# Opening four rows of the first MLP product on half their contraction, with all weight loads ahead of step 4 and step 2 of the attention in two parts

## The chip, the cores and the metric

The kernel runs on one core of a Trainium2 chip. The metric is the device time of one execution in microseconds (us). Most executions of one kernel lie within some tenths of a microsecond of each other, and the change is about an effect of that size, so the number of runs and their range are given with each median.

Engines are called by short names in the profile: PE is TensorE (PEld its weight loads), DVE VectorE, ACT ScalarE, POOL GpSimd, SP or SPq SyncE, which here issues the loads and most stores.

## The reference, cut to what matters

A blocked linear attention with decay (4 batches, 8 heads, 768 positions, head size 64) feeds an MLP with a tanh-GELU:

```python
for b in range(nb):                       # blocks of 64 positions
    intra = einsum('bhic,bhjc->bhij', qb, kb) * Dmask          # decay mask
    intra = einsum('bhij,bhjd->bhid', intra, vb)
    inter = einsum('bhid,bhde->bhie', qb * lam_pow, kv_state)
    out[:, :, sl] = intra + inter
    kv_state = lam_block * kv_state + einsum('bhsd,bhse->bhde', kb_dec, vb)
...
x = attn_out.transpose(0, 2, 1, 3).reshape(3072, 512)          # tokens x model
h = x @ w_in                                                   # 512 -> 2048
g = 0.5 * h * (1 + tanh(c * (h + 0.044715 * h**3)))
return g @ w_out                                               # 2048 -> 512
```

## The kernel before

The attention runs in 24 steps. A step is 256 positions of one batch for one half of the heads (step 0: positions 0 to 255, heads 0 to 3; step 1: the same positions, heads 4 to 7; step 2 and 3: the next 256 positions; and so on). Each step loads q, k and v, casts them to 16 bits (`prep`), transposes q and k on PE and evicts them (`stage_t`), and then multiplies (`region`): scores on PE, times the mask on DVE, times v on PE, plus the running state. Its result, `xT`, holds model dimensions on partitions: the 512 model dimensions are four chunks of 128, and one head half fills two of them. So a token group can enter the MLP only when both of its steps are through.

The MLP is cut into *fillers*, which keep PE busy between the parts of the attention. The first group has 512 tokens, 16 rows of the first product and 16 parts of the second:

```python
def mm1(f0):                       # one row: four products of 512 columns, then GELU on ScalarE
    Hps = ps_M.tile([P, per, N], FP32, tag="M", name="Hps")
    for i in range(per):
        f = f0 + i
        for c in range(NC):
            pin(nc.tensor.matmul(Hps[:, i, :], w_in16[:, c, f * P : (f + 1) * P],
                                 x[:, c, :], start=(c == 0), stop=(c == NC - 1)))
    pin(nc.scalar.activation(out=gT[:, f0 : f0 + per, :], in_=Hps[:], func=AF.Gelu_apprx_tanh))

def mm2(tau, part):                # one part: four products of 512 columns
    ...
    for f in range(4 * part, 4 * part + 4):
        pin(nc.tensor.matmul(O2[tau][:], gT[:, f, tau * P : (tau + 1) * P],
                             w_out16[:, f, :], start=(f == 0), stop=(f == NF - 1)))
    if part < 3:
        return
    ...
    pin(nc.vector.tensor_copy(out=o32[:], in_=o2[:]))      # VectorE empties the output
    pin(nc.sync.dma_start(out=dst, in_=o32[:]))
```

The order of loads on SyncE and the order of work at the start (`idle(n)`: n dummy products on a constant, `R(n, s)`: scores of step n and products of step s, `U(n)`: second state update, `fill(n)`: n fillers):

```python
for s in range(4): load_step(s)
for j in range(4): load_win(j)          # quarters of w_in, 1 MB each
load_wout(0); load_wout(1); load_step(4)
load_wout(2); load_wout(3); load_step(5)
for s in range(6, 9): load_step(s)
...
R(2, 1); stage_t(3); idle(3)
R(3, 2, split=True); idle(3)
R(None, 3)
cast_win(0); U(2); U(3)
...                                      # the other casts
fill(17)                                 # 16 rows and one part
prep(4); cast_wout(2); cast_wout(3); stage_t(4)
fill(3);  R(4, None); U(4); prep(5)
fill(4);  stage_t(5); prep(6)
fill(2);  R(5, 4); U(5)
fill(2);  stage_t(6); prep(7)
fill(2);  R(6, 5); U(6)
...
```

Of the kernel before, what the change touches and what calls it, by code (L numbers as in the profile page):

```python
# [15 lines left out]
def kernel(  # L16
# [12 lines left out]
    P = 128  # L29
# [14 lines left out]
    wst = ctx.enter_context(tc.tile_pool(name="wst", bufs=4))  # L44
# [31 lines left out]
    def load_win(j):  # L76
        t = wst.tile([P, NC, 512], FP32, tag="w32", name=f"wi32_{j}")
        pin(nc.sync.dma_start(out=t[:], in_=moe_w_in[:, j * 512 : (j + 1) * 512].rearrange(
            "(c p) f -> p c f", p=P)))
        wstage[("i", j)] = t  # L80
# [7 lines left out]
    def cast_win(j):  # L88
        t = wstage.pop(("i", j))
        w = 128 if j == 0 else 256  # L90
        for i in range(0, 512, w):
            pin(nc.vector.tensor_copy(out=w_in16[:, :, j * 512 + i : j * 512 + i + w],
                                      in_=t[:, :, i : i + w]))
# [15 lines left out]
    for j in range(4):  # L109
        load_win(j)  # L110
    load_wout(0)
    load_wout(1)
    load_step(4)
    load_wout(2)
    load_wout(3)
    load_step(5)
    for s in range(6, 9):
        load_step(s)
# [61 lines left out]
    def prep(s):  # L180
        half = s % 2
        q32, k32, v32 = ld32.pop(s)
        hs = slice(half * HH, (half + 1) * HH)

        def wide(t):
            return t.rearrange("p j h d -> p h j d")

        def decay(t):
            return t[:, hs, :].unsqueeze(3).to_broadcast([P, HH, 2, D])

        tqk = a16p.tile([P, 2, 2, HH, D], FP16, tag="qk16", name=f"qk16_{s}")
        tq, tk = tqk[:, 0], tqk[:, 1]
        tv = a16p.tile([P, 2, HH, D], FP16, tag="v16", name=f"v16_{s}")
        q_eng = nc.gpsimd if s == 3 else nc.vector
        pin(q_eng.tensor_tensor(wide(tq), q32[:], decay(dq), ALU.mult))  # L195
        if s == 0:
            inverse(halves[0])
            odd(halves[1])
            inverse(halves[1])
        pin(nc.scalar.activation(out=wide(tk), in_=k32[:], func=AF.Copy))  # L200
        pin(nc.gpsimd.tensor_tensor(wide(tv[:]), v32[:], decay(dv), ALU.mult))  # L201
        a16[s] = (tq, tk, tv)
        if s >= FIRST_DMA_T:
            o = qkp.tile([P, 2, 2, 2, P], FP16, tag="qkT", name=f"qkT_{s}")
            pin(nc.sync.dma_start_transpose(out=o[:].rearrange("p a j h t -> p (a j h) t"),
                                            in_=tqk[:].rearrange("p a j h d -> p (a j h d)")))
            qkT[s] = o
        if s >= 6:
            load_ahead(s + 3)

    def stage_t(s):
        if s >= FIRST_DMA_T:
            return
        tq, tk, _ = a16[s]
        Tps = ps_M.tile([P, 2, 2, 2, P], FP16, tag="M", name="Tps")
        for i, t in enumerate((tq, tk)):
            for hp in range(2):
                for j in range(2):
                    pin(nc.tensor.transpose(Tps[:, i, j, hp, :], t[:, j, 2 * hp : 2 * hp + 2, :],  # L219
                                            ident[:]))  # L220
        o = qkp.tile([P, 2, 2, 2, P], FP16, tag="qkT", name=f"qkT_{s}")
        if 1 <= s <= 3:
            pin(nc.scalar.activation(out=o[:], in_=Tps[:], func=AF.Copy))  # L223
        else:
            pin(nc.vector.tensor_copy(out=o[:], in_=Tps[:]))
        qkT[s] = o
# [10 lines left out]
    def region(n, s, split=False):  # L237

        OK = [ps_M.tile([P, 512], FP32, tag="M", name=f"OK{c}") for c in range(2)]
        opened = set()  # L240
# [7 lines left out]
        if n is not None:  # L248
            o = qkT[n]
            _, tk, tv = a16[n]  # L250
            Sps = ps_S.tile([P, 2, 2, 2, P], FP32, tag="S", name="Sps")

            def scores():
                for hp in range(2):
                    for jk in range(2):
                        for hl, c in TILES:
                            pin(nc.tensor.matmul(  # L257
                                Sps[half64(c), hl, hp, jk, :],
                                o[half64(hl), 1, jk, hp, half64(c)],
                                o[half64(hl), 0, :, hp, half64(c)], start=True, stop=True,  # L260
                                skip_group_check=True))

            def products():
                last = (n // 2) % NSB == NSB - 1
                for jk in range(2):
                    for hp in range(2):
                        for c, hl in TILES:
                            if c == 1 and last:
                                continue
                            pin(nc.tensor.matmul(  # L270
                                OK[c][half64(hl), 256 + hp * D : 256 + hp * D + D],
                                tk[half64(c), jk, 2 * hp + hl, :],
                                tv[half64(c), jk, 2 * hp + hl, :],
                                start=start(c, hl), stop=(jk == 1), skip_group_check=True))
                Kps[n] = OK

            if split:
                products()
                update(n, 0)
                scores()  # L280
            else:
                scores()
                products()
            PT = []
            for hps in ([slice(0, 1), slice(1, 2)] if split else [slice(0, 2)]):
                w = hps.stop - hps.start
                t = ptp.tile([P, 2, w, 2, P], FP16, tag=f"PT{w}", name=f"PT_{n}_{hps.start}")
                for src, dst in ([(Sps[:, :, hps.start], t[:, :, 0])] if split else
                                 [(Sps[:].rearrange("p a b c d -> p (a b) c d"),
                                   t[:].rearrange("p a b c d -> p (a b) c d"))]):  # L290
                    pin(nc.vector.tensor_tensor(  # L291
                        dst.rearrange("p a c d -> p a (c d)"),
                        src.rearrange("p a c d -> p a (c d)"),
                        mask[:].unsqueeze(1).to_broadcast([P, 2 * w, 2 * P]), ALU.mult))
                PT += [t[:, :, i] for i in range(w)]
            PTs[n] = PT
        if s is None:
            return
# [4 lines left out]
        for hp in range(2):  # L303
            for jk in range(2):
                for c, hl in TILES:
                    pin(nc.tensor.matmul(  # L306
                        OK[c][half64(hl), hp * P : hp * P + P], tv[half64(c), jk, 2 * hp + hl, :],
                        PT[hp][half64(c), hl, jk, :], start=start(c, hl), stop=False,
                        skip_group_check=True))
        ins = ins_of.pop(s)  # L310
        for c in range(2):
            u = ins[c]
            if u is None:
                continue
            for hp in range(2):
# [13 lines left out]
    ins_of = {}  # L329

    def update(s, c):
# [3 lines left out]
        if c == 0:  # L335
            ins_of[s] = [state[half][1] if sb > 0 else None, None]
# [3 lines left out]
        OK = Kps[s] if c == 0 else Kps.pop(s)  # L340
        K = OK[c][:, 256:384].rearrange("p (hp d) -> p hp d", hp=2)
        t = ucp.tile([P, 2, D], FP32, tag=f"t{half}", name=f"t_{s}_{c}")
        if sb == 0 and c == 0:
            pin(nc.vector.tensor_copy(out=t[:], in_=K))
        else:
            for hp in range(2):
                pin(nc.vector.scalar_tensor_tensor(  # L347
                    t[:, hp, :], state[half][0][:, hp, :],
                    lamu[:, 2 * half + hp : 2 * half + hp + 1], K[:, hp, :], ALU.mult, ALU.add))
        bd = ubp.tile([P, 2, 2, D], FP16, tag=f"u{half}", name=f"u_{s}_{c}")  # L350
        pin(nc.gpsimd.tensor_tensor(  # L351
            bd[:], t[:].unsqueeze(2).to_broadcast([P, 2, 2, D]),
            lumask[:, 2 * half : 2 * half + 2, :].unsqueeze(3).to_broadcast([P, 2, 2, D]),
            ALU.mult))
        state[half] = (t, bd)
        if c == 0:
            ins_of[s][1] = bd
# [6 lines left out]
    def queue_group(g):  # L364
# [3 lines left out]
        x = xT.pop(g)  # L368
# [45 lines left out]
        for f in range(0, NF, per):  # L414
            filler.append(lambda f=f: mm1(f))
# [22 lines left out]
    def R(n, s, split=False):  # L438
        region(n, s, split)
        if s is not None and s % 2 == 1:  # L440
            g, i = group_of[s // 2]
            if i == len(groups[g]) - 1:
                queue_group(g)
        if n is not None and not split:
# [6 lines left out]
    idle(12)  # L451
# [13 lines left out]
    R(1, 0)  # L465
# [3 lines left out]
    U(1)  # L469
    prep(3)  # L470
    R(2, 1)
    stage_t(3)
    idle(3)
    R(3, 2, split=True)
    idle(3)
    R(None, 3)
    cast_win(0)
    U(2)
    U(3)

# [4 lines left out]
    fill(17)  # L485
    prep(4)
    cast_wout(2)
    cast_wout(3)
    stage_t(4)
    fill(3)  # L490
    R(4, None)
    U(4)
    prep(5)
    fill(4)
    stage_t(5)
    prep(6)
    fill(2)
    R(5, 4)
    U(5)
    fill(2)  # L500
    stage_t(6)
    prep(7)
    fill(2)
# [57 lines left out]
```

## Time and profile before

| | before |
|---|---|
| time, median (range, runs) | 214.66 us (214.61 to 215.03, 4 runs) |
| span of the profiled run, and that run's time | 213.5 us, 215.29 us |
| first row of the MLP / fifth row | 19.69 us / 23.61 us |
| first part of the second product | 33.97 us |
| scores of step 5 | 45.47 us |
| tail: last DVE copy through to end of span | 3.25 us |

The tail is counted here and below from the end of the drain record that DVE has behind its last copy, 0.05 us after the copy itself.

The page of the kernel before gives busy time by engine (us, share of the span, instructions) and the chain of work that ended last:

```profile
PE 205.1 (96%) x2118; PEld 107.0 (50%) x2118; DVE 91.3 (43%) x179; ACT 94.2 (44%) x175; POOL 64.2 (30%) x82
...
PE 86%; DMA 7%; SPq 2%; ACT 2%; DVE 1%; issue 0%; ACTq 0%
```

PE is busy for 96% of the span, and the chain runs through it. What is left to win is idle time and dummy products at the start, and the few waits around the first attention steps behind the first MLP group.

### The profile page before, as it was taken

To read this page: it belongs to the slowest core of one execution; us is meant where nothing else is said; L and a number is where in the kernel's file an instruction comes from. 1 tells how busy PE (TensorE), PEld (TensorE's weight loads), DVE (VectorE), ACT (ScalarE), POOL (GpSimd) and SP (SyncE) were. 2 spreads that over 40 slices of the span, in tenths; PEclk is the share of its full clock that TensorE was granted. 3 is DMA by queue.
4 is the path that set the end of the run, shared out by engine and by line. 5 is a ranking of instruction groups with operands and counts; after the bars stand their busy time and mean duration, and the time that the engine had idled before them with its cause. 6 is when DMAs were issued, how large, how long until landed. Compare 5 with 4: busy or idle time off the path is not lost.

```text
span 213.5 us, 5059 instructions
## 1 busy us (share of the span) xinstructions
PE 205.1 (96%) x2118; PEld 107.0 (50%) x2118; DVE 91.3 (43%) x179; ACT 94.2 (44%) x175; POOL 64.2 (30%) x82
## 2 busy tenths in 40 slices
PE   7879999999999999999999999999999999999993
PEld 2444444455875784444455455444455454444452
DVE  4887522478784523740464541363632241100121
ACT  2375774342672471477420577420576211475000
POOL 5493136454582333422421320432420110000000
PEclk9999999999999999999999999999999999999999
DMA  5999999999999999893675673615120012100112
GB/s 135 301 331 391 383 352 370 286 288 325 303 221 223 309 208 253 221 227 71 176 211 144 205 194 69 180 53 150 49 52 0 0 52 98 54 0 0 49 63 86
DMA packets 61879, 37.82 MB, mean 177 GB/s; under 512 B 17696, under 2 KB 54816, under 8 KB 61856
## 3 DMA queue, kind: packets, MB, share of 16 engines
q1 hardware_dynamic: 61696, 37.37, 63.4%
q8 instruction: 16, 0.26, 0.5%
q10 hardware_dynamic: 160, 0.13, 0.2%
q14 instruction: 7, 0.06, 0.1%
HBM read 27.27 MB, written 6.29 MB: 157 GB/s over the span
## 4 chain that ended last, share of the span: by engine, by line
PE 86%; DMA 7%; SPq 2%; ACT 2%; DVE 1%; issue 0%; ACTq 0%
PE Hps L376 38%; PE O2ps L387 34%; DMA k<-in_k_dram 7%; PE Sps L257 3%; PE OK L316 3%; PE OK L306 3%; SPq L67 2%; PE O2ps L407 2%; PE Tps L219 1%; PE OK L270 1%; ACT qkT L223 1%; ACT xT L324 1%; ACT qk L200 1%; DVE PT L291 0%; PE idle L432 0%
## 5 line engine op out<-in xcount | busy, mean ns | idle before, releaser
L376 PE MATMUL Hps<-xT,w_in 128*128 128x512 f16 (+1 forms) x448 | 86.0, 349 | 0.3 <-ACT xT L324 0.3
L387 PE MATMUL O2ps<-w_out,gT 128*128 128x512 f16 x368 | 82.9, 379 | 0.0
L378 ACT ACTIVATE gT<-Hps 128x512 f16<-128x512 f32 x96 | 57.3, 596 | 34.5 <-PE Hps L376 33.7
L376 PEld LDWEIGHTS <-w_in 128*128 128x128 f16 x448 | 43.3, 98 | 38.1 <-issue 0.6
L351 POOL TENSOR_TENSOR u<-t,lumask 128x256 f16<-128x256 f32 x40 | 27.9, 706 | 91.1 <-DVE t L347 64.2
L387 PEld LDWEIGHTS <-gT 128*128 128x128 f16 x368 | 35.3, 98 | 39.7
L291 DVE TENSOR_TENSOR PT<-Sps,mask 128x1024 f16<-128x1024 f32 (+1 forms) x25 | 29.4, 1180 | 45.2 <-PE Sps L257 45.2
L324 ACT ACTIVATE xT<-OK 128x256 f16<-128x256 f32 x48 | 18.3, 451 | 51.3 <-PE OK L316 39.5
L394 DVE COPY o<-O2ps 128x512 f32<-128x512 f32 x23 | 15.8, 690 | 52.6 <-PE O2ps L387 52.5
L201 POOL TENSOR_TENSOR v<-v,dv 128x512 f16<-128x512 f32 x24 | 25.9, 1081 | 4.7 <-DMA v<-in_v_dram 4.6
L195 DVE TENSOR_TENSOR qk<-q,dq 128x512 f16<-128x512 f32 x23 | 19.7, 859 | 6.9 <-DMA q<-in_q_dram 6.9
L200 ACT ACTIVATE qk<-k 128x512 f16<-128x512 f32 x24 | 15.0, 623 | 9.3 <-DMA k<-in_k_dram 9.3
L347 DVE SCALAR_TENSOR_TENSOR t<-t,lamu,OK 128x64 f32<-128x64 f32 x64 | 14.5, 274 | 2.4 <-PE OK L270 1.4
L432 PE MATMUL idle<-ones 128*128 128x512 f16 x30 | 10.2, 479 | 1.5 <-DVE ones L126 1.5
L257 PEld LDWEIGHTS <-qkT 64*64 64x64 f16 x384 | 6.1, 106 | 10.1 <-issue 6.8
L257 PE MATMUL Sps<-qkT 64*64 64x128 f16 x384 | 10.0, 222 | 0.9 <-ACT qkT L223 0.7
L103 POOL CAST w_out<-wo 128x1024 f16<-128x1024 f32 x6 | 6.6, 1113 | 12.4 <-DMA wo<-in_moe_w_out_dram 12.4
L306 PE MATMUL OK<-PT,v 64*64 64x128 f16 x384 | 10.2, 218 | 0.0
L316 PE MATMUL OK<-qkT,u 128*128 128x128 f16 x80 | 8.6, 222 | 0.0
L219 PE MATMUL Tps<-ident,qk 128*128 128x128 f16 x72 | 6.1, 221 | 2.2 <-DVE qk L195 1.0
L306 PEld LDWEIGHTS <-v 64*64 64x64 f16 x384 | 6.8, 108 | 0.9 <-issue 0.8
L219 PEld LDWEIGHTS <-qk 128*128 128x128 f16 x72 | 4.6, 99 | 5.0 <-DVE qk L195 1.8
(34 smaller groups left out, 54.4 us busy)
## 6 DMA issues: line engine op xcount, KB each, us to landing
q<-in_q_dram SPq DMA_DIRECT2D x24, 256.0 KB, 4.7
k<-in_k_dram SPq DMA_DIRECT2D x24, 256.0 KB, 4.9
v<-in_v_dram SPq DMA_DIRECT2D x24, 256.0 KB, 5.2
out_dram<-o SPq DMA_DIRECT2D x23, 256.0 KB, 2.7
wi<-in_moe_w_in_dram SPq DMA_DIRECT2D x4, 1024.0 KB, 11.4
wo<-in_moe_w_out_dram SPq DMA_DIRECT2D x4, 1024.0 KB, 9.4
qkT<-qk SPq DMA_TRANSPOSE x15, 3.4
out_dram<-o SPq DMA_DIRECT2D x1, 96.0 KB, 2.2
```

The lines of the kernel that those rows point to most:

```text
L195: pin(q_eng.tensor_tensor(wide(tq), q32[:], decay(dq), ALU.mult))
L200: pin(nc.scalar.activation(out=wide(tk), in_=k32[:], func=AF.Copy))
L201: pin(nc.gpsimd.tensor_tensor(wide(tv[:]), v32[:], decay(dv), ALU.mult))
L257: pin(nc.tensor.matmul(Sps[half64(c), hl, hp, jk, :], o[half64(hl), 1, jk, hp, half64(c)], o[half64(hl), 0, :, hp, half64(c)], start=True, ...
L291: pin(nc.vector.tensor_tensor(dst.rearrange("p a c d -> p a (c d)"), src.rearrange("p a c d -> p a (c d)"), mask[:].unsqueeze(1).to_broadc ...
L306: pin(nc.tensor.matmul(OK[c][half64(hl), hp * P : hp * P + P], tv[half64(c), jk, 2 * hp + hl, :], PT[hp][half64(c), hl, jk, :], start=star ...
L324: pin(nc.scalar.activation(out=dst[:, :, c * P : (c + 1) * P].rearrange("p hp (t j) -> p hp j t", j=2), in_=OK[c][:, 0:256].rearrange("p ( ...
L351: pin(nc.gpsimd.tensor_tensor(bd[:], t[:].unsqueeze(2).to_broadcast([P, 2, 2, D]), lumask[:, 2 * half : 2 * half + 2, :].unsqueeze(3).to_b ...
L376: pin(nc.tensor.matmul(Hps[:, i, :], w_in16[:, c, f * P : (f + 1) * P], x[:, c, :], start=(c == 0), stop=(c == NC - 1)))
L378: pin(nc.scalar.activation(out=gT[:, f0 : f0 + per, :], in_=Hps[:], func=AF.Gelu_apprx_tanh))
L387: pin(nc.tensor.matmul(O2[tau][:], gT[:, f, tau * P : (tau + 1) * P], w_out16[:, f, :], start=(f == 0), stop=(f == NF - 1)))
L394: pin(nc.vector.tensor_copy(out=o32[:], in_=o2[:]))
```

## The change

The intent is to begin the MLP earlier. Chunks 0 and 1 of the first group's `xT` come from steps 0 and 2, chunks 2 and 3 from steps 1 and 3. Before, PE did dummies while step 3 was still in the attention. Now four rows begin with chunks 0 and 1 as soon as step 2 is through; the first 256 tokens of chunks 2 and 3 (step 1) are added next, the other 256 (step 3) last. For this the first quarter of w_in comes in two loads, half of it cast on ScalarE, step 2 is evicted and masked in two parts, and one state build on GpSimd goes later. All of w_out is loaded ahead of step 4 (six staging buffers in place of four), and more fillers stand ahead of step 4 with fewer between the steps that follow.

The diff, cut to its core:

```diff
-    wst = ctx.enter_context(tc.tile_pool(name="wst", bufs=4))
+    wst = ctx.enter_context(tc.tile_pool(name="wst", bufs=6))
...
     for j in range(4):
-        load_win(j)
-    load_wout(0)
-    load_wout(1)
-    load_step(4)
-    load_wout(2)
-    load_wout(3)
-    load_step(5)
-    for s in range(6, 9):
+        load_win(j, 2 if j == 0 else 1)
+    for j in range(4):
+        load_wout(j)
+    for s in range(4, 9):
         load_step(s)
...
+        def mm1_begin(f, cs):
+            if 0 in cs:
+                first[f] = ps_M.tile([P, N], FP32, tag="M", name="Hps")
+            for c in cs:
+                w = N if c < 2 else SB
+                pin(nc.tensor.matmul(first[f][:, 0:w], w_in16[:, c, f * P : (f + 1) * P],
+                                     x[:, c, 0:w], start=(c == 0), stop=False,
+                                     skip_group_check=True))
+
+        def mm1_end(f):
+            for c in range(2, NC):
+                pin(nc.tensor.matmul(first[f][:, SB:N], w_in16[:, c, f * P : (f + 1) * P],
+                                     x[:, c, SB:N], start=False, stop=True,
+                                     skip_group_check=True))
+            pin(nc.scalar.activation(out=gT[:, f, :], in_=first.pop(f)[:], ...))
...
-    idle(12)
+    idle(11)
...
-    R(2, 1)
+    scores(2)
+    products(2, 1)
+    causal(2, 2)
+    update(2, 0)
+    update(2, 1, "t")
     stage_t(3)
-    idle(3)
-    R(3, 2, split=True)
-    idle(3)
-    R(None, 3)
-    cast_win(0)
-    U(2)
+    idle(2)
+    update(1, 1, "u")
+    products(None, 2)
+    c01, c23 = slice(0, 2), slice(2, 4)
+    cast_win(0, 0, 256, 256, c01)
+    cast_win(0, 256, 512, 256, c01, on_act=True)
+    scores(3)
+    banks = products(3, None)
+    update(3, 0)
+    causal(3)
+    queue_group(0)
+    fill(4)                             # four rows on chunks 0, 1
+    products(None, 3, banks)
+    cast_win(0, 0, 512, 256, c23)
+    update(2, 1, "u")
     U(3)
+    fill(8)                             # their step 1 part, then their step 3 part
...
-    fill(17)
+    fill(12)
+    for j in range(2, 4):
+        cast_wout(j)
+    fill(9)                             # 12 rows and nine parts ahead of step 4
     prep(4)
-    cast_wout(2)
-    cast_wout(3)
     stage_t(4)
-    fill(3)
+    prep(5)
+    fill(2)
     R(4, None)
     U(4)
-    prep(5)
-    fill(4)
+    fill(1)
     stage_t(5)
     prep(6)
-    fill(2)
+    fill(1)
     R(5, 4)
...                                     # and fill(1) for fill(2) around step 6
```

## The prediction

> **What bounds the kernel now.** I read the page first, then the table of stretches, then TensorE (PE) alone in order of time, then VectorE (DVE) in order of time around the first MLP group. The table (columns: stretch and its length, then busy us and instructions per engine, granted clock, DMA share and rate) says where PE is not full:
>
> ```profile
> 16.00:20.60 4.60, 4.07 (x87) 2.23 (x85) 3.20 (x9) 2.56 (x5) 1.80 (x3) 1.00 1.05 388
> 20.60:34.00 13.40, 13.40 (x63) 6.09 (x63) 5.08 (x11) 8.96 (x15) 4.20 (x6) 1.00 1.08 367
> 34.00:53.50 19.50, 18.71 (x217) 9.77 (x216) 12.16 (x22) 7.12 (x12) 10.37 (x12) 1.00 1.03 314
> 53.50:100.00 46.50, 46.50 (x598) 29.29 (x596) 23.89 (x44) 25.62 (x50) 18.70 (x22) 1.00 0.99 228
> ```
>
> From 53.5 us to 205 us PE is busy in every microsecond, so that part only moves as a whole. Time can be won in the 20.6 us ahead of the MLP, where part of PE's busy time is dummy products, and in 34 to 53.5 us, where 0.8 us are visibly idle. PE in order of time (start, length, what, count, idle before):
>
> ```profile
> 16.13 0.81 PE L432 MATMUL idle<-ones 128*128 128x512 f16 x3
> ...
> 18.34 0.81 PE L432 MATMUL idle<-ones 128*128 128x512 f16 x3
> ...
> 19.69 0.59 PE L376 MATMUL Hps<-xT,w_in 128*128 128x512 f16 x2
> 20.59 13.54 PE L376 MATMUL Hps<-xT,w_in 128*128 128x512 f16 x62 [0.31 <-ACT xT L324]
> 33.97 1.03 PE L387 MATMUL O2ps<-w_out,gT 128*128 128x512 f16 x4
> 34.84 0.91 PE L219 MATMUL Tps<-ident,qk 128*128 128x128 f16 x8
> 35.58 2.75 PE L387 MATMUL O2ps<-w_out,gT 128*128 128x512 f16 x12
> ...
> 38.74 3.63 PE L387 MATMUL O2ps<-w_out,gT 128*128 128x512 f16 x16
> 42.91 0.91 PE L219 MATMUL Tps<-ident,qk 128*128 128x128 f16 x8 [0.54 <-DVE qk L195]
> 43.65 1.89 PE L387 MATMUL O2ps<-w_out,gT 128*128 128x512 f16 x8
> 45.47 0.42 PE L257 MATMUL Sps<-qkT 64*64 64x128 f16 x16
> ```
>
> The 62 products from 20.59 to 33.97 pass at 13.38/62 = 0.216 us each: a row (four products of 512 columns) costs 0.863 us, and so does a part of the second MLP product. The group's fifth row therefore starts at 20.59 + 14 x 0.216 = 23.61. The transposes of step 5 wait at 42.9 for q, which waits for its load, as DVE shows:
>
> ```profile
> 21.84 1.52 DVE L92 CAST w_in<-wi 128x1024 f16<-128x1024 f32 x2 [0.51 <-DMA wi<-in_moe_w_in_dram]
> ...
> 42.00 0.85 DVE L195 TENSOR_TENSOR qk<-q,dq 128x512 f16<-128x512 f32 x1 [1.66 <-DMA q<-in_q_dram]
> ```
>
> The first line is the other limit I use: the second quarter of w_in lands at 21.84, whatever PE does.
>
> **What the Trainium skill says.** "TensorE: Matmul & The Clock Gate", Back-to-back issue gap, gives columns/2.4 ns plus 2.5: 216 ns for 512 columns, 109 for 256. The trace agrees for 512 (0.216); for 256, sixteen products take 53.50 to 55.34, 0.115 us each. "PSUM — Partial Sum Buffer", The four PSUM rules, lets a product without the first flag add where columns were written and overwrite elsewhere, so opening a row over all 512 columns and then adding to 256 at a time is sound; no trace shows that yet. "DMA: Bandwidth & Descriptors", Issuing engines are not separate DMA queues, has every load on the same 16 engines; here their share is full up to 90 us, so reordering moves landings but not their sum. In "VectorE: DVE Perf Modes" the errata section puts a fixed cost on each instruction. This trace has 1.22 us for the whole mask multiply and 1.29 for its two halves together.
>
> **The change, part by part.** A first row needs w_in chunks 0 and 1 with head half 0 (steps 0 and 2), chunks 2 and 3 with half 1 (steps 1 and 3). The change opens four rows on chunks 0, 1 while step 3 is still in attention, adds step 1's 256 columns, then step 3's.
>
> (a) PE work. Five dummies go (30 to 25). Eight products of 512 columns become sixteen of 256: 16 x 0.115 - 8 x 0.216 = +0.1 us. That is all that changes in PE's work; the rest is waiting.
>
> (b) Step 2 in two parts. Its transposes are evicted in two ScalarE (ACT) pieces, from 12.69 on; I put 0.6 us on each (a 512-wide ACT pass from PSUM is 0.596), so scores start near 13.3 instead of 13.76 and the mask multiply ends near 15.1. POOL loses one state build ahead of q of step 3 (0.6 us), so step 3's transposes go at about 15.1 instead of 15.67, and their eviction ends near 16.8 instead of 17.36.
>
> (c) Steps 2 and 3. Step 2's products wait for its state on POOL (near 16.7) and end near 17.0; its xT is out near 17.6. Before, it was 19.2. Scores and k-v products of step 3 end near 17.5.
>
> (d) The first half of w_in's first quarter. The whole quarter landed near 19.1 (issued 10.46, 8.7 to landing). At the 2.7 us per MB at which the next quarters follow, the halved load lands 1.35 earlier, near 17.75. DVE then casts 0.4 us ahead of step 3's update and mask multiply, which ends near 19.8. PE opens the rows from 18.2: 8 x 0.216 gives 19.9. Step 3's products end near 20.5, step 1's part at 21.4, step 3's part (xT out near 21.4) at 22.3.
>
> (e) The fifth row needs the second quarter: 21.84 landed, plus 0.68 for half of its cast and a little to hand over, 22.55. So PE, done at 22.3, waits 0.25, and the fifth row starts at 22.55 instead of 23.61: **1.05 us won**, of the 1.3 that PE's own order would give.
>
> (f) Rows 5 to 16 take 12 x 0.863 and end at 32.9. Nine parts of the second product follow up to 40.7. All four w_out quarters now come before step 4; from 27.2 at about 2.8 us per MB they land by about 38.5, each in time for its part. Step 4 lands near 39.5 to 41, step 5 near 42 as before (the bytes ahead of it are the same). Before, 33.97 to 45.47 is 11.5 us for ten parts, two transposes of 0.45 and one set of scores of 0.47, together 10.0: there are **1.5 us of waits** in it, on k of step 4, q and k of step 5. In the new order those operands are ready when PE comes, since five more parts or so lie ahead; these waits go.
>
> (g) A new wait. The fillers between attention steps shrink to one or two. After part 11 (near 42.9) PE has scores 0.47, a part 0.86, transposes 0.45, a part 0.86, and reaches the scores of step 5 at 45.55. DVE must first do, in its order and at its start-to-start pace: two output copies (0.62 each), the mask multiply 1.13, the state update 0.38, a third copy 0.62, the eviction 0.69. With q of step 5 at 42.0 (0.62) that ends at 46.7. PE waits **1.2 us**. At step 6 the same reckoning meets within 0.1 us.
>
> (h) The sum. At the scores of step 5 the new kernel has done 13 parts against 10, so the old place to compare with is 45.47 + 3 x 0.863 = 48.06. New: 46.75. That is 1.05 + 1.5 - 1.2 = **1.3 us won**. One part fewer remains in reserve at each later change of group, but xT is evicted in 0.77 us and a part lasts 0.863, with two products on old chunks after it, so nothing more is lost. 214.68 - 1.3 = 213.4; I leave 0.1 for the extra columns' cost and small waits: **213.5**.
>
> **Rivals.** First: *the new wait eats the gain*. If DVE gets to step 5's eviction later than I reckon (full durations in place of pitches add 0.45 us, and a later q adds to that), it costs 2 us and PE keeps some 0.5: 214.1. The DVE lines between 42 and 50 us, where copies, mask multiply and updates follow without idle, speak for it; that some idle shows at 45.58 speaks against. Second: *the half load does not land early*. DVE takes its instructions in order, and the cast sits ahead of step 3's update and mask multiply. If the first half lands near 19.1, these end at 21.2, the fifth row starts at 23.7, the early gain is gone, and the total gain is 0.2 to 0.3: 214.4. For it: the load is shared by 16 engines and counts as landed with the slowest. Against it: the half behind it needs over a microsecond itself. Third: *the new wait is smaller*, q of step 5 comes earlier than 42.0 or DVE catches up, and 1.05 + 1.5 nearly all stay: 212.3. Against it: the five DVE instructions hang on PE's own part 11, not on a load.
>
> **Range and chances.** The three ways span 212.3 to 214.4 about a centre of 213.5, and a small slip in the start-up could cost 0.5. I give 212.7 to 214.6. Two per cent is 4.3 us, more than all idle time and dummies in question (five dummies, 1.5 us of waits, 1.05), so within 2% has 0.97, faster 0.02, slower 0.01.
>
> **What would show it right or wrong.** In the new trace: 25 dummies; eight 512-wide row products from about 18.2; the fifth row at about 22.5 right behind a cast that ends the DMA's wait at 21.8; no wait of the transposes of steps 4 and 5; one PE wait of about 1.2 us ahead of step 5's scores, released by the DVE eviction, near 46; unbroken PE after 51. If the fifth row starts after 23, step (d) is wrong; if transposes wait for q or k, (f); if step 5's scores don't wait, (g). A break after 53 us would make the whole reckoning wrong.

## The result, and the profile after

| | before | after |
|---|---|---|
| time, median (range, runs) | 214.66 us (214.61 to 215.03, 4) | 214.28 us (214.17 to 214.47, 4) |
| ratio, 95% interval | | 0.998 (0.9962 to 0.9997) |
| span of the profiled run, and its time | 213.5 us, 215.29 us | 212.4 us, 214.17 us |

A ratio here is the mean time of one kernel's fast runs over the mean time of the other's fast runs of the same rounds, so it is not quite the ratio of the medians. The kernel after is correct, and faster by 0.38 us of the 1.2 that were forecast. The two profiled runs differ by 1.1 us and so suggest far more than the times do.

The same two lines of the page, for the kernel after:

```profile
PE 203.6 (96%) x2121; PEld 107.2 (50%) x2121; DVE 88.3 (42%) x178; ACT 94.2 (44%) x177; POOL 65.7 (31%) x82
...
PE 87%; SPq 4%; DMA 3%; DVE 3%; issue 0%; ACT 0%
```

The table of stretches of the kernel after (stretch, length, busy us and instructions of PE, PEld, DVE, ACT and POOL, granted clock, DMA share, GB/s) answers to the first fence of the prediction:

```profile
16.00:20.60 4.60, 3.62 (x65) 1.84 (x64) 2.69 (x6) 2.24 (x6) 1.94 (x4) 1.00 1.06 387
20.60:34.00 13.40, 13.21 (x69) 6.75 (x69) 4.68 (x8) 9.15 (x17) 4.84 (x5) 1.00 1.05 386
34.00:53.50 19.50, 18.68 (x227) 10.70 (x225) 12.88 (x22) 7.07 (x12) 9.68 (x12) 1.00 1.06 309
53.50:100.00 46.50, 46.50 (x590) 28.47 (x587) 22.90 (x43) 26.17 (x51) 18.60 (x21) 1.00 0.99 228
```

In the first stretch PE is now busy for 3.62 us, where it was 4.07, but the time holds row products in place of dummies. In the third there is as much idle time as before, 0.82 against 0.79 us: one wait has come for another. From 53.5 us on nothing has changed. PE in order of time (start, length, what, count, idle before):

```profile
15.01 0.59 PE L462 MATMUL idle<-ones 128*128 128x512 f16 x2
...
17.47 1.90 PE L426 MATMUL Hps<-xT,w_in 128*128 128x512 f16 x8 [0.48 <-DVE w_in L98]
...
19.89 0.27 PE L426 MATMUL Hps<-xT,w_in 128*128 128x256 f16 x1
20.79 0.93 PE L426 MATMUL Hps<-xT,w_in 128*128 128x256 f16 x7 [0.63 <-ACT xT L327]
21.55 1.04 PE L432 MATMUL Hps<-xT,w_in 128*128 128x256 f16 x8
22.42 10.52 PE L380 MATMUL Hps<-xT,w_in 128*128 128x512 f16 x48
32.78 7.93 PE L391 MATMUL O2ps<-w_out,gT 128*128 128x512 f16 x36
40.55 0.61 PE L225 MATMUL Tps<-ident,qk 128*128 128x128 f16 x8
...
44.61 1.03 PE L391 MATMUL O2ps<-w_out,gT 128*128 128x512 f16 x4
46.45 0.42 PE L255 MATMUL Sps<-qkT 64*64 64x128 f16 x16 [0.82 <-DVE qkT L235]
```

The rows open at 17.47 (eight products of 512 columns on chunks 0 and 1), and the fifth row starts at 22.42, where it was 23.61. The transposes of step 4 at 40.55 wait for nothing. The scores of step 5 do wait, 0.82 us, for an eviction on DVE. (The view counts from the modelled end of the product before. In the count that the prediction uses, at 0.216 us for each product from its start, PE could have begun the scores at 45.47, and the wait is 0.98 us.) DVE around that wait, in order of time:

```profile
41.20 0.69 DVE L235 COPY qkT<-Tps 128x1024 f16<-128x1024 f16 x1 [1.84 <-PE Tps L225]
41.80 0.68 DVE L204 TENSOR_TENSOR qk<-q,dq 128x512 f16<-128x512 f32 x1
42.40 1.28 DVE L398 COPY o<-O2ps 128x512 f32<-128x512 f32 x2
43.60 1.22 DVE L272 TENSOR_TENSOR PT<-Sps,mask 128x1024 f16<-128x1024 f32 x1
44.73 0.46 DVE L350 SCALAR_TENSOR_TENSOR t<-t,lamu,OK 128x64 f32<-128x64 f32 x2
45.11 0.68 DVE L398 COPY o<-O2ps 128x512 f32<-128x512 f32 x1
45.72 0.68 DVE L235 COPY qkT<-Tps 128x1024 f16<-128x1024 f16 x1
```

From 41.2 to 46.4 DVE is never idle. The last line is the eviction that step 5 waits for. Three copies of finished outputs (`o<-O2ps`) stand ahead of it in DVE's order.

From the scores of step 6 on PE works without a break: to its last product it takes 159.27 us before and 158.41 after, 0.86 less, for the one part that the new order has done earlier. So the distance that is there at step 6 should be found at the end. It is not. The last DVE copy before and after, each the last line of DVE in order of time:

```profile
209.93 0.29 DVE L410 COPY o<-O2ps 128x128 f32<-128x128 f32 x1 [0.34 <-PE O2ps L407]
```

```profile
208.37 0.29 DVE L414 COPY o<-O2ps 128x128 f32<-128x128 f32 x1 [0.34 <-PE O2ps L411]
```

The copy comes 1.56 us earlier, but the span ends only 1.1 us earlier (213.5 against 212.4). The tail, from the trace's unrounded times, took 3.25 us before and 3.68 us after. So there are two questions: why a trace that is 1.56 us ahead belongs to a kernel that is 0.38 us faster, and what happened in the tail.

### The profile page after: what moved, and what is told of

The parts are those of the page before. It is cut to its first block, busy times and chain, and to the rows that moved or that the text cites. A ratio compares the mean times of both kernels' runs of the same rounds, so it can differ in the third digit from the quotient of the medians.

```text
span 212.4 us, 5060 instructions
## 1 busy us (share of the span) xinstructions
PE 203.6 (96%) x2121; PEld 107.2 (50%) x2121; DVE 88.3 (42%) x178; ACT 94.2 (44%) x177; POOL 65.7 (31%) x82
## 4 chain that ended last, share of the span: by engine, by line
PE 87%; SPq 4%; DMA 3%; DVE 3%; issue 0%; ACT 0%
PE Hps L380 37%; PE O2ps L391 36%; SPq L67 4%; DMA wi<-in_moe_w_in_dram 3%; PE Sps L255 3%; PE OK L319 3%; PE OK L310 2%; PE O2ps L411 2%; PE Hps L426 1%; PE OK L296 1%; PE Tps L225 1%; DVE o L398 1%; DVE qkT L235 1%; DVE PT L272 1%; PE Hps L432 0%
## 5 line engine op out<-in xcount | busy, mean ns | idle before, releaser
L380 PE MATMUL Hps<-xT,w_in 128*128 128x512 f16 (+1 forms) x432 | 82.5, 347 | 0.0
L382 ACT ACTIVATE gT<-Hps 128x512 f16<-128x512 f32 x92 | 54.8, 597 | 27.4 <-PE Hps L380 26.7
L380 PEld LDWEIGHTS <-w_in 128*128 128x128 f16 x432 | 41.8, 98 | 36.0
L357 POOL TENSOR_TENSOR u<-t,lumask 128x256 f16<-128x256 f32 x40 | 29.0, 732 | 90.2 <-DVE t L350 67.2
L194 POOL TENSOR_TENSOR v<-v,dv 128x512 f16<-128x512 f32 x24 | 26.7, 1116 | 5.6 <-DMA v<-in_v_dram 3.9
L204 DVE TENSOR_TENSOR qk<-q,dq 128x512 f16<-128x512 f32 x23 | 18.0, 783 | 10.7 <-DMA q<-in_q_dram 10.6
L462 PE MATMUL idle<-ones 128*128 128x512 f16 x25 | 8.6, 486 | 1.5 <-DVE ones L127 1.5
L108 POOL CAST w_out<-wo 128x1024 f16<-128x1024 f32 x6 | 6.1, 1040 | 10.3 <-DMA wo<-in_moe_w_out_dram 10.3
L98 DVE CAST w_in<-wi 128x1024 f16<-128x1024 f32 (+1 forms) x9 | 5.5, 654 | 3.8 <-DMA wi<-in_moe_w_in_dram 3.8
L296 PE MATMUL OK<-v,qk 64*64 64x64 f16 x320 | 7.0, 192 | 0.0
```

What stands on the lines that cost most here:

```text
L194: pin(nc.gpsimd.tensor_tensor(wide(tv[:]), ld32[s][2][:], decay(dv, s), ALU.mult))
L204: pin(q_eng.tensor_tensor(wide(tq), q32[:], decay(dq, s), ALU.mult))
L357: pin(nc.gpsimd.tensor_tensor(u[:], state[half][:].unsqueeze(2).to_broadcast([P, 2, 2, D]), lumask[:, 2 * half : 2 * half + 2, :].unsqueez ...
```

## The experiments

**Theories.** My first theory was that the change does what was forecast at the front (about 1 us), that the load waits of step (f) stood mainly in the one trace that I had read, and that the tail gives back 0.4 us. Rivals: the new wait on DVE eats the gain; the gain of the front is lost because later work hangs on a load that comes no earlier; what differs is only the chance of when step 2's loads land. The quoted texts name the explanations in their own way.

Twelve experiments ran, all correct: four with the two kernels as they are, and eight with an edit. All timed runs were fast ones, except one of 216.83 us of the kernel `both`, which is left out of its ratio.

### The two kernels again

The kernel before, unedited (no diff), timed beside the kernel before:

> The kernel before, unedited, for its spread and for a second trace. Theory A (the trace that the prediction was worked out from was a slow one: it ran 215.29 us against a median of 214.66, and its loads fell some 0.5 us behind at the issue of step 2's q): this trace has step 2's k landing near 10.9 us instead of 11.5, the fifth row near 23.1 instead of 23.6, a span of 212.8 to 213.0. Rival B (the changed kernel really makes the first loads land earlier): k of step 2 near 11.5 and a span of 213.4 again. Ratio to the kernel before: 1.000 +- 0.001 in both.

Measured: 214.63 us (214.34 to 214.79, 5 runs) against 214.81 (214.55 to 215.19, 11 runs), ratio 0.9989 (0.9977 to 1.0001). The same kernel under another name thus shows a difference of a tenth of a per cent, which is about the size of what is to be explained. Theory A hit the span (212.8 us) and missed its cause: k of step 2 was taken up at 11.82 and the fifth row started at 23.95, both later than in the first trace. Its trace, of a run of 214.62 us, shows another picture from 34 us on than the first one (PE in order of time):

```profile
34.31 1.03 PE L387 MATMUL O2ps<-w_out,gT 128*128 128x512 f16 x4
...
42.53 0.64 PE L219 MATMUL Tps<-ident,qk 128*128 128x128 f16 x8
...
44.83 0.42 PE L257 MATMUL Sps<-qkT 64*64 64x128 f16 x16
```

and its DVE where q of step 5 comes in:

```profile
41.21 0.76 DVE L195 TENSOR_TENSOR qk<-q,dq 128x512 f16<-128x512 f32 x1 [0.54 <-DMA q<-in_q_dram]
```

PE starts the second product 0.34 us *later* than in the first trace and reaches the scores of step 5 0.64 us *earlier*: 10.52 us for the stretch in place of 11.50. The load of q was taken up at 41.21 in place of 42.00. The waits of 1.5 us in step (f) were 0.5 us in this run.

The kernel after, unedited (no diff):

> The changed kernel, unedited, against the kernel before in the same rounds. Theory A: 0.3 to 0.5 us faster again (ratio 0.998), fifth row at 22.4, one wait of 0.8 us ahead of the scores of step 5. Rival (the tail: the first trace of it had 3.7 us from the last copy to the end against 3.3 before): if the tail is again 0.4 us longer than that of the kernel before, the change itself loses there; if both are alike, it was chance.

Measured: 214.57 us (214.30 to 215.04, 6 runs) in the same rounds, ratio 0.9988 (0.9975 to 1.0000). In medians the gain is 0.24 us here, 0.38 in the first measurement. Its trace repeats the first one closely: fifth row at 22.57, scores of step 5 at 46.60, tail 3.66. These rounds alone don't show the gain, since the unedited kernel before came out at the same ratio, 0.9989; the first measurement shows it (0.9962 to 0.9997), and not by much. It is the kernel before whose traces differ.

Two more looks at the kernel before (no diff) were meant to settle how much they differ:

> The kernel before, unedited, a third trace. From the start of the second product to the scores of step 5 it took 11.50 us in the trace that the prediction was worked out from and 10.52 in the second; 10.73 with one dummy less, which changes nothing there. Theory (11.50 was a run in which the load of step 5 came late): 10.4 to 10.9 here. Rival (10.5 was the exception): 11.3 to 11.6. Last copy to end 3.2 in both.

> The same once more, a fourth trace: 10.4 to 10.9 by the theory, 11.3 to 11.6 by the rival.

Measured: 214.74 and 215.30 us, one run each, state unknown. The stretch from the second product to the scores of step 5 was 11.54 and 10.49 us: the rival's figure in the third trace, the theory's in the fourth, so neither is the exception. Together with the kernel `before_idle11` below there are five traces of practically the same kernel:

| trace | fifth row | start of second product | scores of step 5 | stretch | q of step 5 taken up |
|---|---|---|---|---|---|
| before | 23.61 | 33.97 | 45.47 | 11.50 | 42.00 |
| before_again | 23.95 | 34.31 | 44.83 | 10.52 | 41.21 |
| before_third | 23.03 | 33.39 | 44.93 | 11.54 | 41.39 |
| before_fourth | 24.60 | 34.96 | 45.45 | 10.49 | 41.24 |
| before_idle11 | 23.57 | 33.93 | 44.66 | 10.73 | 40.92 |
| mean | 23.75 | 34.11 | 45.07 | 10.96 | 41.35 |

What follows: the stretch holds 10.0 us of work (step (f)), so the waits in it are 0.5 to 1.5 us, about 1.0 in the mean. They are long where PE is early (third) or the load late (first trace), and short where PE is late (fourth): PE meets a load at a time that does not depend on PE. The time at which the fifth row starts also varies, by 1.6 us, in one and the same kernel.

### One half of the change at a time

The front alone: the kernel after, with the load order, the buffers and the fillers of the kernel before.

```diff
-    wst = ctx.enter_context(tc.tile_pool(name="wst", bufs=6))
+    wst = ctx.enter_context(tc.tile_pool(name="wst", bufs=4))
...
-    for j in range(4):
-        load_wout(j)
-    for s in range(4, 9):
+    load_wout(0)
+    load_wout(1)
+    load_step(4)
+    load_wout(2)
+    load_wout(3)
+    load_step(5)
+    for s in range(6, 9):
...
-    fill(12)
-    for j in range(2, 4):
-        cast_wout(j)
-    fill(9)
+    fill(13)
...                                     # and prep(5), fill(3), fill(4), fill(2) as before
```

> Rows opened by halves, step 2 in two parts, dummies cut, w_in's first quarter in two loads; but the old order of the loads, four staging buffers and the old order of fillers from step 4 on. Theory A: the fifth row starts some 0.7 us earlier than in the kernel before, and all of it is lost again at the transposes of step 5, which wait that much longer for q, so 214.5 to 214.7, ratio 0.999 to 1.000. Rival (the two gains add): 0.7 us faster, ratio 0.997.

Measured: 215.33 us (215.19 to 215.41, 5 runs) against 214.81, ratio 1.0022 (1.0009 to 1.0035): slower than the kernel before, which neither theory nor rival had forecast. Its fifth row starts at 22.59, as early as in the kernel after. PE in order of time at the transposes of step 5:

```profile
41.87 0.40 PE L229 MATMUL Tps<-ident,qk 128*128 128x128 f16 x4 [0.43 <-DVE qk L208]
42.76 0.40 PE L229 MATMUL Tps<-ident,qk 128*128 128x128 f16 x4 [0.48 <-ACT qk L213]
```

PE, a microsecond ahead of the mean of the kernel before, waits here for q and then for k of step 5. Its scores come at 44.81, where the before_again trace has 44.83 and the mean of the five 45.07. So of the 1.16 us by which its fifth row is early no more than 0.26 is left behind the load of step 5 (0.2 us of the rest went to a wait for k of step 4), and the longer tail (3.81 us against 3.22 to 3.25) makes the kernel slower than the one before.

The rear alone: the kernel before, with the new load order, six buffers and the new fillers from step 4 on.

```diff
-    load_wout(0)
-    load_wout(1)
-    load_step(4)
-    load_wout(2)
-    load_wout(3)
-    load_step(5)
-    for s in range(6, 9):
+    for j in range(4):
+        load_wout(j)
+    for s in range(4, 9):
...
-    fill(17)
+    fill(16)
+    for j in range(2, 4):
+        cast_wout(j)
+    fill(9)
...                                     # and prep(5), fill(2), fill(1) as in the kernel after
```

> The kernel before with only the weights' loads ahead of step 4 (six staging buffers) and the new order of fillers and attention from step 4 on. Theory A: fifth row as in the kernel before (23.1 to 23.6), the waits of the transposes of steps 4 and 5 (1.5 us) gone, a wait of 0.8 to 1.2 us ahead of the scores of step 5 new: 0.3 to 0.7 us faster, ratio 0.997 to 0.9985. Rival (the new wait takes all of it): ratio 1.000.

Measured: 215.55 us (214.68 to 216.10, 6 runs) against 214.81, ratio 1.0028 (1.0008 to 1.0048): slower, where theory A had a gain of 0.3 to 0.7 us. The trace is of a run of 215.94 us, 0.4 above the median. PE in order of time at the scores of step 5:

```profile
48.56 0.42 PE L253 MATMUL Sps<-qkT 64*64 64x128 f16 x16 [1.50 <-DVE qkT L221]
```

The new wait on DVE is there without the front, and is longer, 1.5 us. The difference is one instruction, the multiply of q of step 5, which takes 1.36 us here and 0.68 in the kernel after (DVE in order of time):

```profile
43.23 1.36 DVE L191 TENSOR_TENSOR qk<-q,dq 128x512 f16<-128x512 f32 x1
```

Here it ran beside POOL's multiply of v (43.00 to 44.04); in the kernel after it was over before that began (43.04). That this meeting made it slow was not tested. With equal work (three parts of 0.863 us added to the mean of the five, 45.07 + 2.59 = 47.66) the scores are 0.9 us late. Neither half wins anything alone; together they win a little. The reading that fits is that the rear takes PE off the load, and the front's lead outweighs the wait that the rear brings; how much of the rear's loss is chance of this one trace is not shown.

### The wait on DVE

The kernel after, with the three outputs of the first group that are copied ahead of the eviction put on ScalarE, whose share of the span is 44%.

```diff
-            pin(nc.vector.tensor_copy(out=o32[:], in_=o2[:]))
+            if g == 0 and tau < 3:
+                pin(nc.scalar.activation(out=o32[:], in_=o2[:], func=AF.Copy))
+            else:
+                pin(nc.vector.tensor_copy(out=o32[:], in_=o2[:]))
```

> The changed kernel with the three output copies of the first group that stand between step 4 and step 5 moved from VectorE to ScalarE. In the two traces of the changed kernel PE reaches the scores of step 5 near 45.5 to 45.6 and starts them at 46.45 and 46.60, behind VectorE's copies (about 0.62 us each), mask multiply, update and eviction. Theory (that wait is a queue on VectorE, and PE's place at 50 us carries to the end): the scores of step 5 start 0.8 to 1.0 us earlier and the time falls by 0.7 to 0.9 against the changed kernel, to 213.5 to 213.8; ratio to the kernel before 0.994 to 0.9955. Rival (a load of q or k of step 5 or 6, or ScalarE, takes over): the wait moves, under 0.3 us won.

Measured: 213.78 us (213.74 to 213.89, 5 runs) against 214.68 (214.38 to 215.28, 11 runs), ratio 0.9958 (0.9946 to 0.9970). DVE in order of time:

```profile
43.56 1.23 DVE L272 TENSOR_TENSOR PT<-Sps,mask 128x1024 f16<-128x1024 f32 x1 [0.80 <-PE Sps L255]
44.70 0.46 DVE L350 SCALAR_TENSOR_TENSOR t<-t,lamu,OK 128x64 f32<-128x64 f32 x2
45.08 0.69 DVE L235 COPY qkT<-Tps 128x1024 f16<-128x1024 f16 x1
```

and PE at the scores of step 5:

```profile
45.84 0.42 PE L255 MATMUL Sps<-qkT 64*64 64x128 f16 x16
```

The copies are gone, the eviction starts at 45.08 in place of 45.72, and PE doesn't wait. From the start of the second product to these scores it is 12.79 us, against 13.67 in the kernel after, and the kernel gains 0.90 us on the one before where the kernel after gained 0.24 to 0.38. This shows that the copies ahead of the eviction were the cause of the wait. Of the 0.88 us that are won at step 5, 0.5 to 0.7 reach the end, less than the 0.7 to 0.9 expected: the scores of step 7 now wait 0.20 us for DVE, at 54.26.

### The tail

SyncE issues half of the last outputs (ScalarE the other half) and then closes the program. Its own records are in the trace, though no view of the profile prints them. Those behind the last DVE copy (record counted from 0, start and end in us from the end of DVE's drain record):

```
after (215 records)         204: 0.03-0.53   205: 2.07-2.25   206: 2.29-2.32   207: 2.69-2.72   208: 2.77-2.80
before (220 records)        209: 0.02-0.54   210: 0.59-2.07   211: 2.11-2.25   212: 2.28-2.31   213: 2.34-2.37
front_only (218 records)    206: -0.04--0.03 207: 0.34-0.81   208: 2.54-2.74   209: 2.78-2.80   210: 2.84-2.87
rear_only (217 records)     206: 0.01-0.53   207: 0.89-2.10   208: 2.16-2.36   209: 2.39-2.42   210: 2.46-2.48
```

Most of these records follow the one before within 0.1 us. But there is a pause of 0.36 to 0.37 us directly ahead of record 207 in the three kernels where it can be seen, whatever that record is: in the kernel after a closing record, in `front_only` the issue of an output, in `rear_only` the long wait for the outputs, which hides most of it. In the kernel before record 207 comes earlier, ahead of the last copy, while SyncE waits anyway. The same is found 128 records earlier: in all fourteen traces SyncE stands for 0.44 to 0.46 us ahead of record 79, be it a load, a transfer or a wait. And in all fourteen the next 8 KB packet of the instruction queue (8192 bytes are 64 for each of 128 records) starts 1.0 to 1.4 us after record 206 has ended. If the position is the cause, five more records ahead of it hide the pause again. That was tried with five unused loads of 32 bytes, early in SyncE's order:

```diff
+    for i in range(5):
+        pad = const.tile([1, H], FP32, name=f"pad{i}", tag=f"pad{i}")
+        pin(nc.sync.dma_start(out=pad[:], in_=lam.unsqueeze(0)))
```

> The changed kernel with five tiny loads more on SyncE's queue (unused copies of lam, behind the load of step 8). In all six traces SyncE pauses 0.3 us or more ahead of its 207th record; in the changed kernel that is between two of its closing waits, after the outputs have landed, and the time from VectorE's last copy to the end is 3.66 to 3.68 us against 3.22 to 3.25 in the kernel before. Theory (the pause belongs to a place in SyncE's instruction stream, and so in the changed kernel it costs the end by chance of its length): with five records more the pause falls into the wait ahead of the last output, last copy to end is 3.2 to 3.3, and the time falls by 0.4 against the changed kernel, ratio to the kernel before 0.996 to 0.9975. Rival (the tail depends on something else of the change): 3.65 again, no gain.

Measured: a tail of 3.07 us in place of 3.68, and 214.05 us (213.93 to 215.26, 6 runs) against 214.68, ratio 0.9984 (0.9963 to 1.0005). The tail answers as expected, and with it the position is shown to matter. The median does too, but two of the six runs took 214.94 and 215.26, so that the ratio says little. Of the 0.61 us that the tail lost, 0.37 is the pause; the other 0.2 us is a last wait that ends at 2.08 in place of 2.25, for which I have no cause.

### The dummies

The change has one dummy fewer in its very first group (11 in place of 12), and the k of step 2 was taken up earlier in the kernel after (10.93 us) than in the first trace of the kernel before (11.48). Did this dummy matter?

```diff
-    idle(12)
+    idle(11)
```

> The kernel before with 11 dummies ahead of step 0 in place of 12. Step 2's k landed at 11.48 and 11.82 in the two traces of the kernel before, 11.70 and 11.55 in the two halves of the change, but 10.93 and 10.99 in the two of the changed kernel. Theory A (one dummy less starts the chain earlier but the loads decide): k of step 2 at 11.4 to 11.9, time as the kernel before. Rival B (the dummy makes the loads go earlier): k near 10.9 to 11.0 and 0.3 to 0.5 us faster.

Measured: 214.94 us (214.47, 214.49, 215.40 and 215.50; 4 runs) against 214.68, ratio 1.0020 (0.9997 to 1.0042). k of step 2 was taken up at 11.43.

The converse, the kernel after with 12:

```diff
-    idle(11)
+    idle(12)
```

> The changed kernel with 12 dummies again. Theory A: k of step 2 near 10.95 still, fifth row near 22.5, time as the changed kernel. Rival B: k near 11.5 to 11.8; even then the fifth row moves by less than 0.4, since the second quarter of w_in decides it; 0.2 us slower at most.

Measured: 214.43 us (214.31 to 214.72, 4 runs) against 214.68, ratio 0.9989 (0.9974 to 1.0003). k of step 2 was taken up at 11.11. The fifth row started at 23.01, 0.6 us later than in the first trace of the kernel after, where theory A said 22.5 and the rival less than 0.4 later; the time answers to theory A.

What follows: no effect of the dummy is seen, though the first of the two intervals is wide enough (up to 1.0042) to hide one of the size of the change. Nor is the early k a mark of the changed kernel, as I had thought: the traces of the kernel before have 10.90 to 11.82 for it, those of the kernel after and its variants 10.93 to 11.87. It differs from run to run of one kernel; what makes these loads differ stays open.

### Putting the two repairs together

First with the five unused loads early, as above, and the three copies on ScalarE (both diffs as shown):

> The changed kernel with both repairs: the three copies on ScalarE and five records more on SyncE. Theory (the two losses are independent and add): scores of step 6 near 49.0 to 49.3 as with the copies alone, last copy to end 3.1 as with the padding alone; time 213.2 to 213.5, ratio to the kernel before 0.993 to 0.9945. Rival (they overlap): 213.7, no better than the copies alone.

Measured: 214.45 us (213.62 to 214.84, five fast runs; a sixth took 216.83) against 214.74, ratio 0.9979 (0.9960 to 0.9997). The tail is 3.08, as hoped, but the times are worse than those of the copies alone. PE in order of time:

```profile
66.50 0.42 PE L259 MATMUL Sps<-qkT 64*64 64x128 f16 x16 [1.14 <-DMA qkT<-qk]
```

PE now waits 1.14 us for the transposing transfer of step 9, which SyncE issues too and which started at 59.5 us here, against 57.6 in `act_copies`. I suspected the loads that had been put early into SyncE's order. The outliers of `sp_pad` may have the same cause; no trace of one was taken.

So the five loads were put where SyncE has time, ahead of the last group's outputs:

```diff
+        if n == NSTEP:
+            for i in range(5):
+                pad = const.tile([1, H], FP32, name=f"pad{i}", tag=f"pad{i}")
+                pin(nc.sync.dma_start(out=pad[:], in_=lam.unsqueeze(0)))
```

> Both repairs again, with the five extra records on SyncE placed ahead of the last group's outputs instead of at 46 us, where they held up the load and the transfer transpose of step 9 in the run before (PE waited 1.1 us for it at 65 us). Theory: no wait of PE for a transposed qkT, scores of step 6 near 49.0, last copy to end 3.1 us instead of 3.65; 213.1 to 213.4, ratio to the kernel before 0.9925 to 0.994. Rival (the copies and the tail don't add): 213.7 as with the copies alone.

Measured: **213.29 us** (212.85 to 213.67, 5 runs) against 214.67 (214.37 to 215.04, 9 runs), ratio 0.9930 (0.9917 to 0.9944). The tail is 3.03 us, and the transposing transfer started at 57.9. This version beats both kernels, by 1.4 us on the one before; the copies alone gave 0.9 and the tail is 0.6 shorter, 1.5 together. It is still within 2% of the kernel before. Its profiled run, the slowest of its five, still has a wait of 0.5 us for such a transfer and one of 0.8 us for v on GpSimd (at 8.61), so that the early place of the padding is not shown to be the whole cause in `both`.

## Why the prediction was right or wrong

**Steps (a) to (e), the front: right in size, not in what limits it.** There are 25 dummies. The rows opened at 17.47 rather than 18.2, since the first half of the quarter was cast from 16.99 on rather than 17.75. Most of that lead was lost again. Step (d) let step 1's part run while step 3's `xT` is evicted, but seven of its eight products started only behind that eviction (ScalarE, 19.97 to 20.73), and PE stood for 0.63 us; why they wait for it is not shown. PE's rows so ended at 22.42 (22.3 was forecast), and the fifth row started at once, where 22.55 was forecast. Step (e) had it wait 0.25 us for the second quarter of w_in. It did not:

```profile
21.21 1.71 DVE L98 CAST w_in<-wi 128x1024 f16<-128x1024 f32 x2
```

DVE came to this cast without waiting for the load and had its first half at 21.90, and in all eight traces with the new front the fifth row follows the last half-width product at 0.11 us, its plain pace. So PE's own chain set the start, not the load, and that 22.55 came so near is in part luck. In eight traces of kernels with the new front it started at 22.42 to 23.01, 22.72 in the mean, against 23.75 in the mean of five traces of the kernel before: 1.03 us earlier; 1.05 was forecast. That rows may be opened over 512 columns and completed over 256 at a time is now shown by the correct results. Rival two, a late half load, is out.

**Step (f), the 1.5 us of waits that go: the step that failed.** The waits do go: the transposes of steps 4 and 5 wait for nothing in the kernel after. What failed is their size. The 1.5 us were read from one trace, of a run of 215.29 us, and subtracted from a median of 214.68. In five traces these waits are 0.5 to 1.5 us, 1.0 in the mean. (The third trace has 1.5 too, in a run of 214.74: one trace was too few, slow or not.) With equal work the stretch from the second product to step 5's scores is 10.96 + 2.59 = 13.55 us before and 13.67 after: 0.1 us is lost in it (1.0 of waits went, 0.98 came, 0.1 was lost besides), where 1.5 - 1.2 = 0.3 was to be won.

**Step (g), the new wait: right in place, cause and order, a fifth too large.** In the prediction's own count it was 0.98 us, not 1.2 (0.82 in the view): PE was there at 45.47 (45.55 was forecast) and its scores came at 46.45 rather than 46.75; DVE went through the very instructions that the step lists. With the copies on ScalarE the wait is gone. So rival three ("both gains nearly all stay") fails, and rival one ("the new wait eats the gain") is right in its size of the total, 0.5 us kept, but not in its reason: the wait was smaller than reckoned.

**Step (h), "nothing more is lost": the other step that failed, by as much, 0.4 us.** The tail is 0.43 us longer in the kernel after, and 0.37 us of it is the pause of SyncE ahead of its record 207, which used to lie in a wait. The new program has 215 SyncE records, the old one 220. Nothing in the profile of before pointed to it; the forecast looked at PE only.

**The sum.** The front +1.0, the stretch -0.1, the tail -0.4: about +0.5 us. Measured were 0.38 and, a second time, 0.24. Most of the rest is in which runs were traced: the five of the kernel before (with `before_idle11`) took 214.88 us in the mean, above its medians (214.63 to 214.81), the three of the kernel after (with `after_idle12`) 214.40, 0.48 less. Against its *own* first trace the forecast came true and more, 1.56 us at the last copy against 1.3: the error was to mix one slow run's trace with the median of others. Within 2% held, and so did the range.

Some things stay open: why the landing of the early loads varies by up to a microsecond between runs of one kernel, what the pauses at records 79 and 207 are (that they belong to the fetch of instructions fits, and is not shown), why step 1's part waits for step 3's `xT`, why the last wait of SyncE ends 0.2 us earlier with five more loads, and whether the outliers of `sp_pad` are late transfers.

## What to carry to other kernels

Before idle time is read off a trace to be subtracted from a median, compare the time of the profiled run with the median, and take a second and a third trace: a wait on a load is as long as PE happens to be early, and need not be there in the next run. A gain ahead of such a load is worth little until the load is moved too, and moving it can put the wait on another engine's queue, so each half of a change may lose where the whole wins. When everything else is tuned, look at the last microseconds on the engine that stores the outputs.

## What the Trainium skill lacked or had wrong

- "TensorE: Matmul & The Clock Gate", Back-to-back issue gap, calls 216 ns for 512 columns the gap of a single product that over-counts in a stream, and gives about 131 ns for a sustained stream with weight loads. Here a sustained stream with weight loads for every product runs at the larger figure: 62 products in 13.38 us, 0.216 us each.
- "Runtime: NRT & Kernel Launch", Instruction fetch mechanics, says that instructions are fetched in blocks of 256 by the sequencer itself, at a cost that is "mostly hidden". It doesn't say that a break at a fixed count of an engine's records can show in the time. Here SyncE paused for 0.36 to 0.37 us ahead of its record 207 in each trace where it could be seen, and for 0.44 to 0.46 us ahead of record 79 in all, 128 records apart and not 256; shifting the count by five shortened the tail from 3.68 to 3.07 us. That the pause is such a fetch is my guess; no run shows it.
- No page that I read says how far the landing of the same load varies from run to run: q of step 5 was taken up between 40.92 and 42.00 us and k of step 2 between 10.90 and 11.82 us in traces of the kernel before. The size of the change's gain lies within that.
